# Single-bank score tiles, halved squares and a new instruction order in an attention and MLP kernel

## The chip, the cores and the metric

The kernel runs on one core of one Trainium2 chip. Its time is the device time of one launch in microseconds (us), the median of several executions. Five engines work side by side, each through its own list of instructions in order: TensorE for matmuls (PE; its weight loads are PEld), VectorE (DVE), ScalarE (ACT), GpSimd (POOL) and SyncE (SP, which here only issues DMAs). An instruction that needs another engine's result waits for a semaphore, and what stands behind it on its engine waits too. [...]

## The reference

Attention with RMS-normalized q and k, for 8 batches of 12 heads, 448 tokens and head size 64; then an MLP on the 3584 tokens of width 768, with inner width 2048:

```python
q_n, k_n = rmsnorm(q, g_q), rmsnorm(k, g_k)        # x / sqrt(mean(x*x) + 1e-6) * g
attn = softmax(scale * q_n @ k_n.T)
x = (attn @ v).transpose(0, 2, 1, 3).reshape(3584, 768)
h = x @ w_in                                       # 768 x 2048
g = h * (1 / (1 + exp(-1.702 * h)))
out = g @ w_out                                    # 2048 x 768
```

Inputs and output are float32; the kernel multiplies in bfloat16.

## The kernel before, in words

**The pieces of work.** Heads are taken in pairs, six pairs per batch, numbered i = 0 to 47. For a pair, `load` fetches q, k and v rows by DMA (112 partitions; 224 KB each). `square` (L1044) squares the rows, on ACT or on GpSimd, `reduce` (L1051) sums the squares on DVE, `seed` and `rsqrt` (L1073, L1084) make the inverse root on DVE and GpSimd, and `norm` (L1097) scales the rows, on GpSimd or DVE. `vcast` (L1104) makes v in bfloat16. The rows are transposed, on PE (`turn_pe`, with `take_q` and `take_k` behind it) or by a DMA (`turn_dma`, with `scale_q` behind it: the KQ scalings). Then `score` (L1157) multiplies q by k into a score tile, `expo` (L1173) takes exponentials on ACT, `values` (L1183) multiplies them by v into the one `o` bank, with a column of ones that gives the sum, and `divide` (L1196) divides on DVE, which frees the `o` bank. The quotient is transposed into `xt`, on PE (`back_pe`, `take_x`) or by DMA.

For a batch, `first` (L1398) multiplies `xt` by w_in in 16 blocks of 128 columns, `tanh` (L1411, ACT) and `gate` (L1415, DVE) form g, and the second product, by w_out, is done per pair of batches and 128 tokens. Most of it is done as a Strassen-like scheme of seven products (P1 to P7) of operands that `add_up` (L1485, DVE) has summed; `product` (L1492) is one of them, 8 matmuls 384 wide. `copy_out` (ACT) and `copy_out_v` (DVE) scale a sum into SBUF, `add_out` (L1513, DVE) adds a further product, and `store` (L1445) writes it out, on SP's queue or, for the very last tokens, partly on ACT's. The last two batches' first products are done jointly in the same manner, after attention has ended: `joint_product` (L1738), `part_copy`, `part_add`, `gelu` (L1750 to L1764).

**PSUM.** Two score tiles `sc0`, `sc1` of two banks each, one `o` bank and three `w` banks. Before attention ends, the products share `w` banks only. Once it has ended (task `late`, L1842), the four halves of the two score tiles are put to use as four more banks for the products: `banks` is a list of seven from which `bank()` takes what the planner chose.

**The order.** It isn't written out by hand. Each piece of work is a task in `_Order` (from L27), with an engine, an assumed duration, what it depends on, the slots that it takes ("w", "sc", "o", "osb", "sums"), and a key. `run` plays the tasks through on the assumed durations; whenever an engine is free, it emits the ready task of the lowest key. The emission order on each engine is the program; the chip then runs it with semaphores, whatever the real durations. Keys are in a table `KEYS`, the earliest times of loads in `AT`, and `ON` names the tasks that use their second engine (GpSimd for a square, DVE for a norm, ACT for a KQ scaling). `FINAL` (L1537) is the list of the last products, ending with E8 and E4.

**Zero matmuls.** `fill` (L1018) is called ahead of each PE task with the idle time that the plan sees, and puts in matmuls of zeros, 256 columns wide, into the `w` bank not yet in use; it is switched off when the number of `w` banks grows (`widen`), which is when the first projection begins. There are 92 of them.

Of the kernel before, what the change touches and what calls it, by code (L numbers as in the profile page):

```python
# [26 lines left out]
class _Order:  # L27
# [36 lines left out]
    def run(self):  # L64
# [60 lines left out]
        while emitted < len(self.tasks):  # L125
            for eng, q in ready.items():
                while q and free[eng] <= now:
# [24 lines left out]
                    for name, n in best.widen or ():  # L152
                        self.slots[name][0] = n
                        self.fill = None
# [71 lines left out]
    'Lg': 0.22, 'g': 55.26, 'gT': 30.23, 'gG': 70, ('L', 0, 0): 0.37, ('L', 0, 1): 0.13, ('L',  # L226
    0, 2): 17.62, ('S', 0, 0): -40, ('R', 0, 0): 17.66, ('S', 0, 1): -37.12, ('R', 0, 1): 56.72,
    ('Q', 0): -38.13, ('N', 0, 0): -12.18, ('N', 0, 1): 14.86, ('V', 0): 56.98, ('T', 0, 0):
    12.94, ('T', 0, 1): -21.61, ('KQ', 0): 70, ('K', 0): 65.88, ('L', 1, 0): 7.61, ('L', 1, 1):
    7.62, ('L', 1, 2): 1.46, ('S', 1, 0): -39.85, ('R', 1, 0): 30.33, ('S', 1, 1): 0.22, ('R',  # L230
    1, 1): 30.34, ('Q', 1): -39.63, ('N', 1, 0): -13.05, ('N', 1, 1): -14.01, ('V', 1): 70,
    ('T', 1, 0): 6.24, ('T', 1, 1): 13.57, ('KQ', 1): 69.99, ('K', 1): 18.15, ('L', 2, 0): 17.9,
    ('L', 2, 1): 38.14, ('L', 2, 2): -5.44, ('S', 2, 0): -33.18, ('R', 2, 0): 13.95, ('Q', 2):
    -38.13, ('N', 2, 0): -29.82, ('N', 2, 1): -13.56, ('V', 2): -13.57, ('T', 2, 0): -21.6,
    ('T', 2, 1): 16.29, ('KQ', 2): 70, ('K', 2): 62.97, ('L', 3, 0): 41.06, ('L', 3, 1): 9.24,
    ('L', 3, 2): 43.15, ('S', 3, 0): -38.12, ('R', 3, 0): 65.09, ('Q', 3): -34.18, ('N', 3, 0):
    -12.87, ('N', 3, 1): -26.87, ('V', 3): 69.95, ('T', 3, 0): 11.11, ('T', 3, 1): 11.69, ('KQ',
    3): 56.73, ('K', 3): 20.74, ('L', 4, 0): 18.91, ('L', 4, 1): -19.56, ('L', 4, 2): 15.83,
    ('S', 4, 0): 0.95, ('R', 4, 0): 67.9, ('Q', 4): -34.27, ('N', 4, 0): 20.82, ('N', 4, 1):
    -17.57, ('V', 4): -11.3, ('T', 4, 0): -3.0, ('T', 4, 1): -2.97, ('KQ', 4): -11.72, ('K', 4):  # L240
    69.48, ('L', 5, 0): 22.36, ('L', 5, 1): -18.14, ('L', 5, 2): 17.7, ('S', 5, 0): -10.17,
    ('R', 5, 0): 70, ('Q', 5): -37.13, ('N', 5, 0): 24.39, ('N', 5, 1): -26.27, ('V', 5): 15.01,
    ('T', 5, 0): -12.89, ('T', 5, 1): -11.92, ('KQ', 5): 60.78, ('K', 5): 59.31, ('L', 6, 0):
    15.46, ('L', 6, 1): -18.15, ('L', 6, 2): -3.94, ('S', 6, 0): -16.71, ('R', 6, 0): -7.33,
    ('N', 6, 0): -16.52, ('N', 6, 1): -10.48, ('V', 6): 6.19, ('T', 6, 0): 10.28, ('T', 6, 1):
    23.05, ('KQ', 6): 0.72, ('K', 6): 3.84, ('L', 7, 0): 38.54, ('L', 7, 1): 15.83, ('L', 7, 2):
    -4.28, ('S', 7, 0): -24.47, ('R', 7, 0): 3.83, ('N', 7, 0): 6.2, ('N', 7, 1): 6.21, ('V',
    7): -9.14, ('T', 7, 0): -39.98, ('T', 7, 1): -38.38, ('KQ', 7): -6.41, ('K', 7): 0.85, ('L',
    8, 0): -1.72, ('L', 8, 1): 11.56, ('L', 8, 2): 10.08, ('S', 8, 0): -24.91, ('R', 8, 0):
    -6.41, ('Q0', 8): 32.07, ('Q', 8): 28.01, ('N', 8, 0): 5.71, ('N', 8, 1): -8.0, ('V', 8):  # L250
    -12.74, ('T', 8, 0): 13.67, ('T', 8, 1): 47.73, ('KQ', 8): 0.59, ('K', 8): -0.49, ('L', 9,
    0): -10.64, ('L', 9, 1): 10.1, ('L', 9, 2): 45.1, ('S', 9, 0): 26.07, ('R', 9, 0): 6.92,
    ('N', 9, 0): -6.74, ('N', 9, 1): -10.36, ('V', 9): 13.05, ('T', 9, 0): 44.4, ('T', 9, 1):
    5.86, ('KQ', 9): 18.33, ('K', 9): -6.72, ('L', 10, 0): -12.09, ('L', 10, 1): 38.53, ('L',
    10, 2): 9.25, ('S', 10, 0): -24.13, ('R', 10, 0): 4.83, ('N', 10, 0): -4.44, ('N', 10, 1):
    -6.78, ('V', 10): -10.35, ('T', 10, 0): 26.56, ('T', 10, 1): 9.68, ('KQ', 10): 37.6, ('K',
    10): 0.88, ('L', 11, 0): -9.36, ('L', 11, 1): -16.64, ('L', 11, 2): -26.52, ('S', 11, 0):
    -10.35, ('R', 11, 0): -6.55, ('Q0', 11): -11.27, ('Q', 11): -18.03, ('N', 11, 0): 0.65,
    ('N', 11, 1): 1.38, ('V', 11): -4.19, ('T', 11, 0): 7.07, ('T', 11, 1): -11.77, ('KQ', 11):
    -12.98, ('K', 11): 30.09, ('L', 12, 0): -5.03, ('L', 12, 1): -35.43, ('L', 12, 2): -20.7,  # L260
    ('S', 12, 0): 46.96, ('R', 12, 0): -6.72, ('N', 12, 0): 36.31, ('N', 12, 1): 26.26, ('V',
    12): 24.25, ('T', 12, 1): 68.34, ('KQ', 12): 9.67, ('L', 13, 0): -35.76, ('L', 13, 1):
    -13.65, ('L', 13, 2): -12.08, ('S', 13, 0): 19.67, ('R', 13, 0): -11.91, ('N', 13, 0):
    -5.48, ('N', 13, 1): 10.21, ('V', 13): 35.01, ('T', 13, 1): 50.14, ('KQ', 13): 29.64, ('L',
    14, 0): -28.77, ('L', 14, 1): -33.63, ('L', 14, 2): -23.28, ('S', 14, 0): -32.54, ('R', 14,
    0): -6.68, ('Q0', 14): 14.59, ('Q', 14): 42.35, ('N', 14, 0): 42.36, ('N', 14, 1): 17.66,
    ('V', 14): 52.1, ('T', 14, 1): 68.52, ('KQ', 14): 30.13, ('L', 15, 0): -10.21, ('L', 15, 1):
    -21.03, ('L', 15, 2): -10.86, ('S', 15, 0): 21.43, ('R', 15, 0): 0.71, ('N', 15, 0): 17.26,
    ('N', 15, 1): -14.78, ('V', 15): 17.91, ('T', 15, 1): 69.44, ('KQ', 15): -3.57, ('L', 16,
    0): -10.28, ('L', 16, 1): -2.32, ('L', 16, 2): -23.28, ('S', 16, 0): 27.33, ('R', 16, 0):  # L270
    31.04, ('N', 16, 0): 15.29, ('N', 16, 1): -10.33, ('V', 16): 21.01, ('T', 16, 1): 64.02,
    ('KQ', 16): 17.87, ('L', 17, 0): -11.13, ('L', 17, 1): 4.77, ('L', 17, 2): -26.53, ('S', 17,
    0): 55.55, ('R', 17, 0): 34.56, ('Q0', 17): 38.18, ('Q', 17): -14.77, ('N', 17, 0): 17.28,
    ('N', 17, 1): -14.76, ('V', 17): 21.85, ('T', 17, 1): 54.96, ('KQ', 17): 18.94, ('L', 18,
    0): -10.24, ('L', 18, 1): -18.65, ('L', 18, 2): 60.64, ('S', 18, 0): 8.24, ('R', 18, 0):
    -0.11, ('N', 18, 0): 18.68, ('N', 18, 1): 18.68, ('V', 18): 22.61, ('T', 18, 1): 19.87,
    ('KQ', 18): 13.42, ('L', 19, 0): 65.93, ('L', 19, 1): 68.74, ('L', 19, 2): 57.38, ('S', 19,
    0): 68.06, ('R', 19, 0): 19.11, ('N', 19, 0): 13.7, ('N', 19, 1): 18.69, ('V', 19): 24.79,
    ('T', 19, 1): 27.31, ('KQ', 19): 20.75, ('L', 20, 0): 49.44, ('L', 20, 1): 49.43, ('L', 20,
    2): 18.36, ('S', 20, 0): 47.45, ('R', 20, 0): -7.1, ('Q0', 20): 17.6, ('Q', 20): 17.74,  # L280
    ('N', 20, 0): 18.63, ('N', 20, 1): 19.13, ('V', 20): 10.89, ('T', 20, 1): 23.29, ('KQ', 20):
    19.79, ('L', 21, 0): 49.88, ('L', 21, 1): 54.32, ('L', 21, 2): 21.44, ('S', 21, 0): 32.39,
    ('R', 21, 0): 24.48, ('N', 21, 0): 40.58, ('N', 21, 1): 20.67, ('V', 21): 9.73, ('T', 21,
    1): 20.87, ('KQ', 21): 24.17, ('L', 22, 0): 54.3, ('L', 22, 1): 45.12, ('L', 22, 2): 23.02,
    ('S', 22, 0): 9.37, ('R', 22, 0): 18.5, ('N', 22, 0): 40.59, ('N', 22, 1): 22.19, ('V', 22):
    19.73, ('T', 22, 1): 21.96, ('KQ', 22): 25.44, ('L', 23, 0): 20.78, ('L', 23, 1): 17.14,
    ('L', 23, 2): 21.94, ('S', 23, 0): 19.12, ('R', 23, 0): 19.39, ('Q0', 23): 37.96, ('Q', 23):
    58.13, ('N', 23, 0): 42.56, ('N', 23, 1): 21.37, ('V', 23): 12.12, ('T', 23, 1): 19.53,
    ('KQ', 23): 27.37, ('L', 24, 0): 27.32, ('L', 24, 1): 23.46, ('L', 24, 2): 19.89, ('S', 24,
    0): 15.36, ('R', 24, 0): 20.63, ('N', 24, 0): 24.12, ('N', 24, 1): 26.27, ('V', 24): 9.99,  # L290
    ('T', 24, 1): 14.3, ('KQ', 24): 34.67, ('L', 25, 0): 21.43, ('L', 25, 1): 21.42, ('L', 25,
    2): 19.52, ('S', 25, 0): 22.92, ('R', 25, 0): 29.14, ('N', 25, 0): 20.8, ('N', 25, 1):
    30.38, ('V', 25): 13.2, ('T', 25, 1): 24.46, ('KQ', 25): 27.87, ('L', 26, 0): 21.46, ('L',
    26, 1): 21.76, ('L', 26, 2): 19.55, ('S', 26, 0): 11.3, ('R', 26, 0): 3.81, ('Q0', 26):
    10.43, ('Q', 26): 11.29, ('N', 26, 0): 33.52, ('N', 26, 1): 32.94, ('V', 26): 36.87, ('T',
# [562 lines left out]
def kernel(  # L858
# [138 lines left out]
    ps_sc = pool("ps_sc", 1, space=PSUM)  # L997
    ps_o = pool("ps_o", 1, space=PSUM)
    ps_w = pool("ps_w", 1, space=PSUM)

    od = _Order()
    for name, n in (("sc", 2), ("o", 1), ("w", 2), ("th", 3), ("osb", 5)):
        od.slot(name, n)
# [931 lines left out]
```

## Time and the profile before

| | |
|---|---|
| median of 3 executions | 423.13 us (422.65 to 424.16) |
| profiled execution | 425.17 us |
| its span, first to last instruction | 423.4 us |
| PE's idle share | 4% |
| mean granted clock of PE | 0.996 |
| traffic with HBM | 45.61 MB read, 11.01 MB written |

The span is what the trace covers; the execution's own time is 1.8 us more. In the trace, a line of the timeline gives the start and length in us, the engine, the source line (L1403 is line 1403 of the kernel), the operation, what it writes and reads, and in brackets how long the engine stood idle ahead of it and what ended that. A group of equal instructions in a row is one line with xcount. The groups of the page give the busy time, the mean in ns and the idle time before them. The costliest on PE are the first product (L1403, 121.2 us in 672 matmuls), the second (L1497) and the attention products (L1170, L1191: 1280 matmuls of 65 columns in 58.7 us); on ACT the exponentials (L1178, 168 of 915 ns); on DVE the reductions (L1058, 50 of 1171 ns), the gates (L1425, 96 of 615 ns) and the divisions (L1202, 96 of 425 ns); on GpSimd the norms (L1100, 61 of 1115 ns) and squares (L1046, 27.1 us in 14).

### The profile page before, as it was taken

The page shows a single profiled execution, that of the slowest core. Times are in us where ns is not written, and L with a number is a line of the kernel's source. Part 1 is how long each engine was busy: PE and PEld are TensorE (multiplying, and loading weights), DVE is VectorE, ACT ScalarE, POOL GpSimd, SP SyncE. Part 2 cuts the span into 40 slices and gives each one's busy share as a digit, 9 for nine tenths or more (in the row PEclk, how much of TensorE's full clock was granted, in tenths as well). Part 3 has the DMA queues.
Part 4 walks back from the last instruction along what each step waited for, and adds up shares of the span by engine and source line. Part 5 has one row for each costly group of instructions (what it writes and reads, how often), then busy time and mean ns, then how long its engine had stood idle before and what let it go on. Part 6 is the DMA issues. An engine that isn't in the chain of part 4 may idle for free.

```text
span 423.4 us, 10002 instructions
## 1 busy us (share of the span) xinstructions
PE 406.6 (96%) x3845; PEld 238.7 (56%) x3845; DVE 324.7 (77%) x647; ACT 295.4 (70%) x435; POOL 173.4 (41%) x252
## 2 busy tenths in 40 slices
PE   7899989998999999999999999999999999999995
PEld 5658866554555555554555554555555654545663
DVE  4877878879999888888788869998666897557432
ACT  3898585889878578867897768858887625763221
POOL 4965986581545175807537364662300000000000
PEclk9999998999999999999999999999999999999999
DMA  9999999966385899695974878546441231001323
GB/s 207 245 245 245 256 238 249 239 165 132 88 185 128 161 227 212 119 240 148 212 171 119 179 198 223 130 111 161 112 110 33 70 77 49 3 0 24 89 76 112
DMA packets 101556, 63.38 MB, mean 150 GB/s; under 512 B 54916, under 2 KB 101508, under 8 KB 101508
## 3 DMA queue, kind: packets, MB, share of 16 engines
q1 hardware_dynamic: 93712, 55.88, 56.0%
q0 software_dynamic: 7296, 6.29, 9.1%
q8 instruction: 30, 0.49, 0.5%
q10 hardware_dynamic: 500, 0.57, 0.4%
q14 instruction: 18, 0.15, 0.1%
HBM read 45.61 MB, written 11.01 MB: 134 GB/s over the span
## 4 chain that ended last, share of the span: by engine, by line
PE 69%; DMA 13%; DVE 11%; ACT 3%; issue 2%; SPq 0%; DVEq 0%; ACTq 0%
PE w L1403 21%; PE w L1497 18%; PE o L1191 10%; PE sc L1170 8%; DMA rows<-in_q_dram 6%; DMA rows<-in_k_dram 5%; PE sc L1497 5%; PE w L1433 4%; PE sc L1744 2%; DMA late<-in_k_dram 2%; PE w L1744 2%; DVE late L1488 1%; DVE obs L1202 1%; DVE ssq L1058 1%; DVE att L1758 1%
## 5 line engine op out<-in xcount | busy, mean ns | idle before, releaser
L1178 ACT ACTIVATE att<-sc 112x896 bf16<-112x896 f32 x168 | 145.8, 915 | 37.2 <-PE sc L1170 36.5
L1403 PE MATMUL w<-xt,w_in_s 128*128 128x448 bf16 (+1 forms) x672 | 121.2, 327 | 0.7 <-DVE g L1425 0.4
L1403 PEld LDWEIGHTS <-w_in_s 128*128 128x128 bf16 x672 | 61.2, 98 | 44.8 <-issue 9.9
L1191 PEld LDWEIGHTS <-att 112*128 112x128 bf16 x1536 | 62.7, 98 | 30.0 <-issue 8.2
L1100 POOL TENSOR_TENSOR row<-rows,rs 112x512 bf16<-112x512 f32 x61 | 66.7, 1115 | 11.1 <-DMA qk<-row 9.2
L1413 ACT ACTIVATE th<-w 128x448 f32<-128x448 f32 x96 | 51.8, 546 | 24.3 <-PE w L1403 23.4
L1425 DVE SCALAR_TENSOR_TENSOR g<-th,w 128x448 bf16<-128x448 f32 x96 | 57.9, 615 | 12.2 <-ACT th L1413 11.8
L1058 DVE TENSOR_REDUCE ssq<-sq 112x16 f32<-112x1024 f32 (+1 forms) x50 | 58.4, 1171 | 10.9 <-ACT sq L1049 7.8
L1191 PE MATMUL o<-vx,att 112*128 112x65 bf16 x1280 | 58.7, 194 | 4.2 <-DVE obs L1202 3.8
L1113 POOL TENSOR_TENSOR vx<-rows,ones 112x512 bf16<-112x512 f32 x20 | 21.9, 1095 | 66.9 <-PE o L1191 59.2
L1170 PE MATMUL sc<-qk 64*128 64x448 bf16 (+1 forms) x360 | 47.3, 342 | 0.4 <-DVE qk L1130 0.2
L1046 POOL TENSOR_TENSOR sq<-rows 112x1024 f32<-112x1024 f32 (+1 forms) x14 | 27.1, 1934 | 43.2 <-DMA rows<-in_k_dram 17.3
L1202 DVE TENSOR_TENSOR obs<-o,rcp 112x256 bf16<-112x256 f32 x96 | 40.8, 425 | 3.3
L1497 PEld LDWEIGHTS <-g 128*128 128x128 bf16 x296 | 27.2, 98 | 21.1 <-issue 4.7
L1497 PEld LDWEIGHTS <-late 128*128 128x128 bf16 x304 | 27.5, 97 | 19.2 <-issue 2.9
L1049 ACT ACTIVATE sq<-rows 112x1024 f32<-112x1024 f32 (+1 forms) x32 | 32.3, 1016 | 5.5 <-DMA rows<-in_q_dram 2.8
L1497 PE MATMUL w<-w_out_s,g 128*128 128x384 bf16 x152 | 28.7, 326 | 0.0
L1497 PE MATMUL w<-w_out_s,late 128*128 128x384 bf16 x152 | 28.6, 326 | 0.0
L1201 DVE RECIPROCAL rcp<-o 112x4 f32<-112x4 f32 x96 | 17.0, 177 | 14.8 <-PE o L1191 14.5
L1100 DVE TENSOR_TENSOR row<-rows,rs 112x512 bf16<-112x512 f32 x27 | 22.7, 841 | 2.2 <-POOL rs L1093 2.0
L1497 PE MATMUL w<-late 128*128 128x384 bf16 x128 | 24.3, 326 | 0.1
L1180 ACT ACTIVATE att<-sc 112x896 bf16<-112x896 f32 x24 | 20.5, 916 | 1.2 <-PE sc L1170 1.1
(130 smaller groups left out, 505.5 us busy)
## 6 DMA issues: line engine op xcount, KB each, us to landing
rows<-in_q_dram SPq DMA_DIRECT2D x44, 224.0 KB, 3.8
rows<-in_k_dram SPq DMA_DIRECT2D x43, 224.0 KB, 4.3
rows<-in_v_dram SPq DMA_DIRECT2D x42, 224.0 KB, 3.4
w_in_s<-in_moe_w_in_dram POOLq DMA_DIRECT2D x4, 768.0 KB, 17.0
w_out_s<-in_moe_w_out_dram POOLq DMA_DIRECT2D x4, 768.0 KB, 21.2
out_dram<-osb SPq DMA_DIRECT2D x10, 168.0 KB, 2.9
out_dram<-osb SPq DMA_DIRECT2D x14, 120.0 KB, 2.1
out_dram<-osb SPq DMA_DIRECT2D x11, 144.0 KB, 2.6
```

Source lines behind the costliest of these rows:

```text
L1046: nc.gpsimd.tensor_tensor(out=sq[i % N_SQ][:SS, part], in0=raw[turn(i, N_RAW, K_RAW)][:SS, part], in1=raw[turn(i, N_RAW, K_RAW)][:SS, part ...
L1049: nc.scalar.activation(out=sq[i % N_SQ][:SS, part], in_=raw[turn(i, N_RAW, K_RAW)][:SS, part], func=ACT.Square)
L1058: nc.vector.reduce_sum(out=ssq_of[g0][:SS, i - g0, part], in_=sq[i % N_SQ][:SS, part], axis=AX.X)
L1100: eng.tensor_tensor(out=row_ring[i % N_QKN][:SS, gi].rearrange("p n (h d) -> p h n d", h=2), in0=raw[turn(i, N_RAW, K_RAW)][:SS, gi], in1= ...
L1170: nc.tensor.matmul(sc[:, hp, j * SH:j * SH + n], lhsT=qkw[r, k0:k0 + WIN], rhs=qk[r, 0, qs], start=True, stop=True)
L1178: nc.scalar.activation(out=att[:SS, t, :, :S], in_=sc, func=ACT.Exp)
L1191: nc.tensor.matmul(os_[u, w][:, x, :], lhsT=att_of(u)[:SS, kc, hp, qs * SS:qs * SS + WIN], rhs=vx_ring[turn(i, N_V, K_V)][:SS, hp, kc, :], ...
L1202: nc.vector.tensor_tensor(out=to[:SS, :, w, :] if h is None else to[:SS, :2].rearrange("p n h d -> p (n h) d"), in0=o[:SS, :, :D], in1=rcp ...
L1403: nc.tensor.matmul(gps[b, m][:, j * SH:j * SH + n], lhsT=w_in_s[:, ki, f * 128:(f + 1) * 128], rhs=xT[b][:, ki, lo:lo + n], start=(ki == 0 ...
L1413: nc.scalar.activation(out=th[:, :], in_=gps[b, m][:, :S], func=ACT.Tanh, scale=0.851)
L1425: nc.vector.scalar_tensor_tensor(out=g_of[b // 2][:, f:f + len(g), lo:lo + n], in0=view(ths.pop((b, m))[:, :]), scalar=1.0, in1=view(gps.p ...
L1497: nc.tensor.matmul(held[to], lhsT=lhs[:, ko, :], rhs=y[:, ko, :], start=first and ko == 0, stop=ko == NK - 1, skip_group_check=not first)
```

## The change

1. **Banks.** The score tiles' pool is closed when attention ends, and four tiles of one bank each, `b0` to `b3`, take the place of the four halves (`part_banks`). The pool of the score tiles is made last, so that it can be closed first.
2. **Zero matmuls.** `fill` is no longer switched off. The matmuls are 240 wide; until 14 us of planned time and until 45 us the number follows the idle time, with other divisors; later it puts some in only where the plan sees more than 0.9 us of idle time, and into an open bank. The built program has 103.
3. **Squares.** A square on GpSimd is two instructions of 112x512 (q and k apart) in place of one of 112x1024. The pairs whose square is on GpSimd are 15 and a half of one before, 16 after.
4. **Last product.** E4 becomes E9: the last product is done in two column halves of 192, 8 matmuls each; the first half is copied out by ACT and the second by DVE, and each is stored by itself.
5. **A new order.** All of `KEYS`, `AT` and `ON` have other values. Counted in the built programs: norms on DVE 27 before and 23 after, on GpSimd 61 and 65; V conversions on DVE 17 and 19, on GpSimd 20 and 18 (of the main buffers); KQ scalings on DVE 22 and 24, on ACT 14 and 12; copies of products on DVE 20 and 16 (osb), and eight more on ACT.
6. `joint_product` looks up its operand only for the product that it issues; the work is the same.

The diff without the tables:

```diff
@@ -151,7 +151,6 @@
                     for name, n in best.widen or ():
                         self.slots[name][0] = n
-                        self.fill = None
                     if eng == "PE" and self.fill:
                         self.fill(now - free[eng], now)
...
-    ps_sc = pool("ps_sc", 1, space=PSUM)
     ps_o = pool("ps_o", 1, space=PSUM)
     ps_w = pool("ps_w", 1, space=PSUM)
+    scores = ctx.enter_context(ExitStack())
+    ps_sc = scores.enter_context(tc.tile_pool(name="ps_sc", bufs=1, space=PSUM))
...
+    def part_banks():
+        scores.close()
+        ps_b = pool("ps_b", 1, space=PSUM)
+        banks[3:] = [ps_b.tile([128, 512], FP32, tag=f"b{j}", name=f"b{j}") for j in range(4)]
+
...
-        n = idle * FILL / 213 if now < 14000.0 else idle * FILL_GAPS / 110
-        for _ in range(int(n)):
-            nc.tensor.matmul(banks[2][:, :256], lhsT=ident[:, :], rhs=zeros[:, :],
+        if now < 14000.0:
+            n = idle * FILL / 200
+        elif now < 45000.0:
+            n = idle * FILL_GAPS / 103
+        else:
+            n = (idle - 400.0) * FILL_GAPS / 103 if idle > 900.0 else 0.0
...
+        for _ in range(n):
+            nc.tensor.matmul(banks[j][:, :240], lhsT=ident[:, :], rhs=zeros[:, :240],
                              start=True, stop=True)
...
         if ("S", i, part.start) in ON:
-            nc.gpsimd.tensor_tensor(out=sq[i % N_SQ][:SS, part], in0=raw[turn(i, N_RAW, K_RAW)][:SS, part],
-                                    in1=raw[turn(i, N_RAW, K_RAW)][:SS, part], op=ALU.mult)
+            for g in range(part.start, part.stop):
+                nc.gpsimd.tensor_tensor(out=sq[i % N_SQ][:SS, g], in0=raw[turn(i, N_RAW, K_RAW)][:SS, g],
+                                        in1=raw[turn(i, N_RAW, K_RAW)][:SS, g], op=ALU.mult)
             return
...
-                   alt=("POOL", 1700 / len(parts) + 200, False),
+                   alt=("POOL", 1050 * (part.stop - part.start), False),
...
-    def store(bp, tm, hf):
+    def store(bp, tm, hf, part=None):
...
-                in_=osb[r:r + n, :HALF])
+                in_=osb[r:r + n, part])
...
+    def product_part(to, x, y, cols):
+        lhs = sum_of[x] if x in sum_of else tokens(*x)
+        for ko in range(NK):
+            nc.tensor.matmul(held[to][:, cols], lhsT=lhs[:, ko, :], rhs=y[:, ko, cols],
+                             start=False, stop=ko == NK - 1, skip_group_check=True)
+
+    def copy_part(frm, bp, tm, hf, cols, by_v):
+        to, x = half_of(bp, tm, hf)[:, cols], held[frm][:, cols]
+        if by_v:
+            nc.vector.tensor_scalar(out=to, in0=x, scalar1=SCALE[bp], scalar2=None, op0=ALU.mult)
+        else:
+            nc.scalar.mul(to, x, SCALE[bp])
...
-                   "E5 C7 E6 C4 C3 E7 E8 E4")
+                   "E5 C7 E6 C4 C3 E7 E8 E9")
...
+        def p4_last():
+            nonlocal done, last
+            hf = HALF // 2
+            for j in range(2):
+                cols = slice(j * hf, (j + 1) * hf)
+                od.add((*P(4), j), "PE", 8 * 82,
+                       lambda cols=cols: product_part(a, A(3), T4, cols), now_key(),
+                       deps=[last, X(3)] + term(3), lat=250)
+                last = (*P(4), j)
+                done += 8 * 82
+                name = ("U", *at[1], 0, 0)[:5 - j]
+                od.add(name, "ACT" if j == 0 else "DVE", 310 if j == 0 else 320,
+                       lambda j=j, cols=cols: copy_part(a, *at[1], 0, cols, j), now_key() - 3,
+                       deps=[last], takes=("osb", [("D", *at[1], 0)]) if j == 0 else None)
+                od.add(("D", *at[1], 0, j) if j == 0 else ("D", *at[1], 0), "SP", 900,
+                       lambda cols=cols: store(*at[1], 0, cols), now_key() + 1,
+                       deps=[name], moves=300.0)
...
-            od.add("late", "none", 0, lambda: None, 0, widen=[("w", len(banks))],
+            od.add("late", "none", 0, part_banks, 0, widen=[("w", len(banks))],
```

## The prediction

> **What bounds the kernel now.** I read the page first, then busy time by stage, then the timeline where a stage loses time. The page's first part:
>
> ```profile
> PE 406.6 (96%) x3845; PEld 238.7 (56%) x3845; DVE 324.7 (77%) x647; ACT 295.4 (70%) x435; POOL 173.4 (41%) x252
> ```
>
> PE is the bound, and the change keeps its work (3753 matmuls in both built programs, fillers apart), so only PE's idle and slow time can be won. The stages (start:end, length, then PE, PEld, DVE, ACT, POOL busy, granted clock, DMA share, GB/s):
>
> ```profile
> 0.00:60.00 60.00, 54.41 (x678) 41.83 (x679) 44.05 (x99) 44.35 (x66) 43.14 (x67) 1.00 1.12 239
> 60.00:70.00 10.00, 7.89 (x74) 5.48 (x72) 7.71 (x14) 7.76 (x12) 9.23 (x15) 0.83 1.22 247
> 70.00:335.00 265.00, 261.74 (x2582) 145.28 (x2581) 220.47 (x448) 206.82 (x289) 120.89 (x171) 1.00 0.69 157
> 335.00:418.80 83.80, 82.52 (x518) 46.11 (x516) 52.45 (x89) 36.03 (x70) 0.18 (x1) 1.00 0.20 54
> 418.80:423.40 4.60, 0.02 (x1) 0.00 (x0) 0.00 (x0) 0.49 (x1) 0.00 (x0) 0.98 0.33 99
> ```
>
> At a saturated 239 to 247 GB/s, loads set the pace to about 60 us (fillers hide idle PE time). From 70 us PE is 98.6% busy; the tail is 4.6 us. 60 to 70 us is the worst:
>
> ```profile
> 58.49 1.06 ACT L1049 ACTIVATE sq<-late 112x1024 f32<-112x1024 f32 x1 [1.06 <-DMA late<-in_k_dram]
> 61.33 1.22 DVE L1058 TENSOR_REDUCE ssq<-sq 112x16 f32<-112x1024 f32 x1 [0.46 <-ACT sq L1049]
> 62.47 0.17 DVE L1201 RECIPROCAL rcp<-o 112x4 f32<-112x4 f32 x1
> 63.16 0.56 PE L1191 MATMUL o<-vx,att 112*128 112x65 bf16 x12 [2.11 <-DVE obs L1202]
> 64.13 1.81 PE L1403 MATMUL w<-xt,w_in_s 128*128 128x224 bf16 x12
> ```
>
> A k load lands late; the squares wait, the reduce waits for them, and the divide that frees the one `o` bank is queued behind the reduce on DVE. PE stands 2.11 us: in PE's order nothing lies between two `o` blocks here. Then the clock is halved for 3.4 us (granted 0.60 over 64 to 68 us; twelve L1403 matmuls take 1.81 us, 1.31 elsewhere): about 1.7 us lost.
>
> In two later holes a GpSimd square holds up a DVE instruction:
>
> ```profile
> 191.90 1.89 POOL L1046 TENSOR_TENSOR sq<-rows 112x1024 f32<-112x1024 f32 x1 [10.18 <-DVE ssq L1058]
> 192.08 1.76 DVE L1079 TENSOR_SCALAR rs<-ssq 112x48 int32<-112x48 int32 x1
> 194.91 0.68 PE L1191 MATMUL o<-vx,att 112*128 112x65 bf16 x16 [0.88 <-DVE obs L1202]
> ...
> 280.35 2.51 POOL L1046 TENSOR_TENSOR sq<-rows 112x1024 f32<-112x1024 f32 x1 [2.99 <-DMA rows<-in_k_dram]
> 281.02 2.38 DVE L1488 TENSOR_TENSOR late<-g,late 128x1024 bf16<-128x1024 bf16 x1
> 284.01 0.68 PE L1191 MATMUL o<-vx,att 112*128 112x65 bf16 x16 [0.63 <-DVE obs L1202]
> ```
>
> Undisturbed, L1079 takes 0.19 us and L1488 0.69; here each ends with the square, and the next divide and PE are late.
>
> In the joint stage (from 335 us) PE loses 3.3 us in twelve pieces of 0.2 to 0.6:
>
> ```profile
> 359.15 0.52 ACT L1755 COPY osb<-sc 128x448 f32<-128x448 f32 x1
> 359.73 0.73 PE L1744 MATMUL sc<-xt,rows 128*128 128x448 bf16 x3
> 359.73 0.85 PEld L1744 LDWEIGHTS <-rows 128*128 128x128 bf16 x5 [0.35 <-issue]
> ```
>
> These matmuls begin as the copy ends (359.15+0.52 = 359.67); in the built program they write one half of the two-bank score tile, and the copy reads the other.
>
> [...]
>
> **Single banks after attention.** The built program of before has 16 waits in the joint and final stages whose named reader is in the other half of the tile; after has none, and PE's waits in that region fall from 70 to 63. Between the last write of a tile and its next one, PE has 0 to 0.65 us of other work eleven times; after, 0.65 at the least and mostly 2.27. A reader needs about 0.6 us (copy 0.52 and its signal), so about eight of the twelve holes, at 0.25 each, go: **−2.0**. Both ends: 0, if the next wait (part_add at L1758, which waits for the ACT copy) takes their place, and −3.3, all of it. The other edit in that function, a product operand chosen when emitted, moves no work: 0.
>
> **Squares in two.** 15 squares of 112x1024 (2003 ns mean) and one half become 32 halves; the one half in the trace took 1.04 us. GpSimd: 16×2.08 against 15×2.00+1.04, +2 us, and +4×1.1 for norms moved to it, at 41% busy: hidden by its idle time of 250 us. A blocked DVE instruction waits at most 1.04 us instead of 2.0: the holes of 0.88+0.16 and 0.63+0.18 us shrink by about 0.6 each: **−1.2**, bounds −1.9 (both gone) and +0.5 (the other places[...]).
>
> **New order.** DVE gives up four norms (0.84 each) and four copies (0.56) and takes two V reductions (0.68) and two KQ scalings (0.44 at most): 3 to 4 us less, at 77% busy; ACT takes eight copies (0.49) and gives up two of 14 KQ scalings (0.68). Neither bounds. PE work between consecutive `o` blocks falls below 0.5 us at four places before (0 at the stall; 0.38 at 95 and at 229 us), at one after, early: **−0.4** (0.2 to 0.4 us at each of two, part of it taken by waits elsewhere). At 60 us 1.55 us of other PE work now lies between, but it waits for exps and tanhs that ACT runs behind the same two squares, and the last k load of the pair is SP load 41, not 40: 224 KB at 245 GB/s, 0.9 us later. Of 1.55 minus 0.9 I take **−0.4**. The half-clock window follows or not by chance: half of 1.7, **−0.9** (0 to −1.7). The first score comes about 1 us earlier (two first norms on DVE at 0.84 instead of GpSimd at 1.1), but the loads set the pace to 58 us: 0. A searched order has holes of its own that order lists do not show; between 70 and 335 us before loses 3.3 us, and I allow half of that again: **+1.5** (0 to +4).
>
> **Zero matmuls.** 92×256 columns become 103×240, 100 of them before about 45 us, where PE waits anyway (0.1 us each hidden by load waits; if a load came sooner, up to 0.3 us late). Three are at about 96 us, where PE stands 0.74 us for transposes: **0**. The first waits on ACT, so a late ACT there would pass through: +0.3 at worst.
>
> **Last product in halves.** Eight matmuls of 384 (1.30 us) become sixteen of 192 (1.32). In the built program the ACT copy of half one waits for all sixteen, and the DVE copy of half two for the ACT copy: same bank. From 0.49 us (384 wide) and 0.53 (448) I estimate 0.33 for ACT; from 0.555, 0.36 for DVE. The second large store is issued about 0.3 us later (two issues of 0.38 on ACT's queue), with half the bytes (168 KB land in 2.3 us, 72 in 1.9): −0.2. **+0.1**, bounds −0.5 and +0.5.
>
> **Sum.** −2.0−1.2−0.4−0.4−0.9+1.5+0.1 = −3.3 us in the span. The profiled execution took 425.17 us around a span of 423.4; the runs' median, 423.13, is lower than either sum suggests, so I take the difference from the median: **419.8 us**.
>
> **The rivals.**
> A, the forecast: 419.8; own range 417.5 to 421.5; chance 0.46.
> C, the block at 60 us dissolves: the 2.11 us wait and the half-clock window both go, −3.8 in place of −1.3: 417.3, and 416.5 with fewer new holes. For it: the 1.55 us between the `o` blocks. Against: the later k load. 0.13.
> B, holes move: the joint stage's waits pass to the DVE adds (half of −2.0 lost), and the new order's holes are +3 instead of +1.5: 419.8+1.0+1.5 = 422.3. For it: PE at 98.6% leaves little to win. 0.20, of which 0.07 is faster by over 0.3%.
> D, slower: at about 60 us the late k load (0.9) holds ACT's squares, the exps and tanhs behind them (two of 0.92) come late, PE has only their products left, and a second half-clock window (1.7) follows. That is 4.4 us against −2.0 from the sum without its 60 us terms: 425.5. It decides from 3.3 us of added stall there (2.0 won elsewhere plus 1.27). For it: ACT is in order and both squares stand together; DMA is saturated until 70 us. Against: PE has more work queued, DVE some 3 us less. 0.21.
> That the edits don't do what they say holds for the tail alone (halves without overlap), and is priced.
>
> **How the numbers follow.** 0.3%, 1.27 us, is about what a measurement of this kernel can tell from no change; same is 421.9 to 424.4. Faster: 0.46+0.13+0.07 = 0.66; same 0.13; slower 0.21. The range goes from 416.0, just below C, to 425.0, within D; about 0.05 lies below and 0.11 above.
>
> **What would show it.** Joint stage: no matmul that writes a score bank waits for a copy of another, and PE loses about 1.3 us from 335 us on instead of 3.3. Squares of 1.04 us, and no DVE instruction over about 1.1 us longer than usual behind one. Around 60 us: a PE wait of about 1.5 us, and the granted clock shows whether the half-clock window came. At the end: about 4.7 us from the last matmul. The prediction is wrong if loads end later than 60 us by several load times, if the middle stage loses over 5 us, or if the joint stage's waits come back on DVE.

## The result

The kernel after takes 417.88 us (median of 4, 417.36 to 418.74), the kernel before beside it 423.64: a ratio of 0.986, interval 0.9818 to 0.9902. Measured once more, in the study below, it took 420.20 (median of 6) against 424.01, a ratio of 0.9909 (0.9890 to 0.9928). The two intervals share 0.989 to 0.990; 0.9 to 1.4% faster, 4 to 6 us, is what the two together support.

The profiled execution took 417.67 us, its span is 415.9. PE is busy for 404.9 us of it (97%). Its worst stretch before, from 60 to 70 us (start:end, length; PE, PEld, DVE, ACT and POOL busy, granted clock, DMA share, GB/s):

```profile
60.00:70.00 10.00, 9.68 (x120) 6.88 (x117) 8.99 (x19) 8.66 (x14) 8.46 (x12) 1.00 1.22 249
```

PE is busy 9.68 us there instead of 7.89, at full clock instead of 0.83. The timeline there (here and below, lines between the ones shown are left out):

```profile
57.59 2.00 ACT L1068 ACTIVATE sq<-late 112x1024 f32<-112x1024 f32 x2
58.68 2.35 DVE L1077 TENSOR_REDUCE ssq<-sq 112x16 f32<-112x1024 f32 x2
59.28 0.68 PE L1210 MATMUL o<-vx,att 112*128 112x65 bf16 x16
59.80 1.31 PE L1422 MATMUL w<-xt,w_in_s 128*128 128x224 bf16 x12
61.15 0.42 DVE L1221 TENSOR_TENSOR obs<-o,rcp 112x256 bf16<-112x256 f32 x1
61.25 0.56 PE L1189 MATMUL sc<-qk 64*128 64x448 bf16 x4
61.74 0.56 PEld L1210 LDWEIGHTS <-att 112*128 112x128 bf16 x16 [0.37 <-DVE obs L1221]
```

Neither these reduces nor ACT's squares show a wait. Twelve first-product matmuls (1.31 us, where twelve took 1.81 at 64 us in before) and four score matmuls (0.56) now lie between two `o` blocks, and the second block waits 0.37 us instead of 2.11.

The same DVE instruction as at 192 us before, behind a square in two halves of 1.02 us each (187.95 to 189.99), and the `o` block after it:

```profile
188.13 0.91 DVE L1098 TENSOR_SCALAR rs<-ssq 112x48 int32<-112x48 int32 x1
189.76 0.68 PE L1210 MATMUL o<-vx,att 112*128 112x65 bf16 x16
```

It takes 0.91 us instead of 1.76 (0.19 undisturbed), and PE doesn't wait. The place in the joint stage that was at 359 us:

```profile
353.61 0.53 ACT L1808 COPY osb<-b 128x448 f32<-128x448 f32 x1
353.98 0.73 PE L1797 MATMUL b<-xt,rows 128*128 128x448 bf16 x3
```

The matmuls into one bank begin 0.16 us before the copy of another ends (353.61+0.53). And the tail:

```profile
412.02 0.33 ACT L1532 ACTIVATE att<-b 128x192 f32<-128x192 f32 x1 [2.13 <-PE b L1524]
412.38 0.87 ACTq L1475 DMA_DIRECT2D out_dram<-att  x2
412.39 0.36 DVE L1530 TENSOR_SCALAR att<-b 128x192 f32<-128x192 f32 x1 [1.12 <-ACT att L1532]
```

The halves follow one another, as the built program said: all matmuls, ACT's copy, DVE's copy. Still the span ends 2.65 us after the last issue (413.25 to 415.9), where it ended 3.64 after it before (419.76 to 423.4).

**Lost time by stage.** For comparing fourteen traces I use one number: the length of a stage less what its real matmuls take when they follow each other without a gap (0.19 us for 448 columns and 0.1625 for 384, as far as their starts lie apart in the trace of the kernel after; 0.039 for 65, the mean of fifteen steps of 0.033 within an `o` block and one of 0.127 to the scores behind it; a wide score matmul, which has only 64 rows and starts within some 4 ns of a second one in the trace, counts half; about 379 us in all). Stages are cut at equal amounts of that work: 34, 46 and 300 us, which is about 55, 70 and 335 us of time. Other weights move a whole column of the table; the differences between its rows hardly change. In us, one profiled execution each:

| kernel | loads (to 34) | block (34 to 46) | middle (to 300) | joint, final | tail | span |
|---|---|---|---|---|---|---|
| before | 21.5 | 3.7 | 11.3 | 3.4 | 4.6 | 423.4 |
| after | 21.6 | 0.4 | 10.0 | 1.1 | 3.9 | 415.9 |
| after_again | 23.3 | 0.6 | 10.5 | 1.0 | 3.9 | 418.3 |
| a_two_bank | 23.0 | 0.7 | 10.9 | 3.5 | 3.9 | 420.9 |
| a_whole_sq | 22.2 | 0.7 | 11.3 | 1.1 | 4.4 | 418.5 |
| a_quarter_sq | 21.1 | 0.6 | 10.0 | 1.0 | 3.9 | 415.7 |
| a_e4 | 23.9 | 0.4 | 10.4 | 1.1 | 4.2 | 418.9 |
| a_no_late_zero | 20.7 | 0.5 | 11.1 | 1.0 | 3.9 | 416.2 |
| a_order_alone | 21.6 | 1.0 | 10.6 | 3.5 | 4.7 | 420.3 |
| b_one_bank | 21.3 | 3.5 | 12.3 | 1.7 | 4.5 | 422.2 |
| b_half_sq | 20.5 | 1.1 | 10.2 | 3.4 | 4.2 | 418.3 |
| b_work_before_o | 21.3 | 2.6 | 12.0 | 3.4 | 4.6 | 422.9 |
| b_zeros_in_stall | 22.2 | 5.8 | 11.5 | 3.4 | 4.6 | 426.4 |
| b_square_first | 21.7 | 12.3 | 13.1 | 3.4 | 4.6 | 434.0 |

From before to after: block −3.3, middle −1.3, joint and final −2.3, tail −0.7, loads +0.1. But these are single executions. The same program in `after` and `after_again` differs by 2.4 us, 1.7 of it in the load stage; the eight traces with the new order lost 20.7 to 23.9 us there. The block of before has a half-clock stretch (granted 0.50 from 64.81 to 68.23 us) worth about 1.7 us; only 37 of before's 102 runs have a mean granted clock under 0.998. The profiled execution of before was 0.9 to 1.5 us above four of the kernel's medians (2.0 above that of its first three runs), that of after near the low end of its ten runs. Of the 7.5 us between the two spans, then, 1.5 to 3.5 are the executions.

### The profile page after: what moved, and what is told of

It reads as the page before. It is cut to its first block, busy times and chain, and to the rows that moved or that the text cites. A ratio compares the mean times of both kernels' runs of the same rounds, so it can differ in the third digit from the quotient of the medians.

```text
span 415.9 us, 10074 instructions
## 1 busy us (share of the span) xinstructions
PE 404.9 (97%) x3864; PEld 240.0 (58%) x3864; DVE 319.8 (77%) x644; ACT 297.0 (71%) x437; POOL 175.5 (42%) x270
## 4 chain that ended last, share of the span: by engine, by line
PE 80%; DMA 7%; DVE 4%; ACT 3%; issue 2%; POOL 2%; SPq 0%; DVEq 0%; POOLq 0%; ACTq 0%
PE w L1422 22%; PE w L1517 21%; PE o L1210 11%; PE sc L1189 9%; PE b L1517 4%; PE b L1797 4%; DMA rows<-in_q_dram 4%; PE w L1797 4%; PE w L1452 3%; DMA late<-in_v_dram 3%; ACT att L1199 2%; POOL row L1119 1%; DMA rows<-in_k_dram 1%; DVE late L1508 1%; ACT L902 1%
## 5 line engine op out<-in xcount | busy, mean ns | idle before, releaser
L1119 POOL TENSOR_TENSOR row<-rows,rs 112x512 bf16<-112x512 f32 x65 | 69.0, 1083 | 31.8 <-DMA qk<-row 14.7
L1132 POOL TENSOR_TENSOR vx<-rows,ones 112x512 bf16<-112x512 f32 x18 | 19.0, 1057 | 54.5 <-PE o L1210 41.8
L1517 PEld LDWEIGHTS <-late 128*128 128x128 bf16 x304 | 28.0, 98 | 21.4 <-issue 4.4
L1065 POOL TENSOR_TENSOR sq<-rows 112x512 f32<-112x512 f32 x28 | 28.6, 1039 | 24.5 <-DMA rows<-in_q_dram 10.5
L1517 PEld LDWEIGHTS <-g 128*128 128x128 bf16 x288 | 26.3, 98 | 19.3 <-issue 3.6
L1517 PE MATMUL w<-w_out_s,late 128*128 128x384 bf16 x144 | 27.0, 326 | 0.1
L1517 PE MATMUL w<-late 128*128 128x384 bf16 x136 | 25.6, 326 | 0.1
L1109 POOL TENSOR_TENSOR t<-rs 112x48 f32<-112x48 f32 x28 | 9.5, 339 | 29.4 <-DVE rs L1098 28.3
## 6 DMA issues: line engine op xcount, KB each, us to landing
w_out_s<-in_moe_w_out_dram POOLq DMA_DIRECT2D x4, 768.0 KB, 20.5
```

Source lines behind the costliest of these rows:

```text
L1119: eng.tensor_tensor(out=row_ring[i % N_QKN][:SS, gi].rearrange("p n (h d) -> p h n d", h=2), in0=raw[turn(i, N_RAW, K_RAW)][:SS, gi], in1= ...
L1517: nc.tensor.matmul(held[to], lhsT=lhs[:, ko, :], rhs=y[:, ko, :], start=first and ko == 0, stop=ko == NK - 1, skip_group_check=not first)
```

## The experiments

Names in a_ are the kernel after with something undone, names in b_ the kernel before with something done. All ratios are to the kernel before on the same chip; its median was 424.04, 424.31 and 424.01 us in the three groups (40, 51 and 11 runs), so 0.1% is 0.42 us. The third group (a_quarter_sq, a_no_late_zero, b_square_first and the kernel after again) ran on another chip than the first two, so kernels of different groups are compared by their ratios.

**Banks, undone and done alone.** (A bank is here a tile of 128x512 float32 in PSUM, where matmuls leave their sums.)

```diff
-            od.add("late", "none", 0, part_banks, 0, widen=[("w", len(banks))],
+            od.add("late", "none", 0, lambda: None, 0, widen=[("w", len(banks))],
```

a_two_bank:

> The kernel after, with the four halves of the two-bank score tiles in place of the four single-bank tiles; nothing else changes, and the order of every engine stays. Built, it has 19 waits of product matmuls on a reader of the other half (the kernel after: 0, before: 21). Theory of the banks: the holes of 0.2 to 0.3 us come back in the joint and final stages, PE loses about 3.0 us there instead of 1.3, time +1.5 to +2.0 us against the kernel after. Rival (the new order alone keeps readers ahead of writers): PE has other work between the two writes, and the time moves by less than 0.5 us.

b_one_bank has the opposite edit, with the score pool made last:

> The kernel before with single-bank tiles once attention has ended, and nothing else. Theory of the banks: PE's loss from 335 us to its last matmul falls from 3.3 to about 1.5 us, time -1.8 against the kernel before, all of it after 343 us. Rival (the new order is needed for it): under -0.5. The stall at 60 us is untouched: about 2.1 us of waiting for the divided o block, and the half clock after it when it comes.

a_two_bank took 422.18 us, ratio 0.9946 (0.9926 to 0.9967). By the ratios that is 1.6 us over the second measurement of the kernel after (0.9909) and 3.6 over the first (0.986); joint and final stages lost 3.5 us instead of 1.0. Its timeline where the kernel after has no wait:

```profile
357.00 0.53 ACT L1808 COPY osb<-sc 128x448 f32<-128x448 f32 x1
357.59 0.73 PE L1797 MATMUL sc<-xt,rows 128*128 128x448 bf16 x3
```

b_one_bank took 421.87 us, 0.9938 (0.9918 to 0.9958), 2.2 us under before by the medians and 2.6 by the ratio; joint and final stages 1.7 instead of 3.4. At the same point of the program:

```profile
359.36 0.53 ACT L1761 COPY osb<-b 128x448 f32<-128x448 f32 x1
359.73 0.73 PE L1750 MATMUL b<-xt,rows 128*128 128x448 bf16 x3
```

With the halves, the matmuls begin 0.06 us after the copy ended (357.53); with banks of their own, 0.16 before it ends (359.89). So what the theory of the banks expects shows in both orders, at about the forecast size. The new order isn't needed for it.

**Squares.** a_whole_sq puts the single instruction of 112x1024 back, b_half_sq splits it in the kernel before:

```diff
-            for g in range(part.start, part.stop):
-                nc.gpsimd.tensor_tensor(out=sq[i % N_SQ][:SS, g], in0=raw[...][:SS, g], in1=raw[...][:SS, g], op=ALU.mult)
+            nc.gpsimd.tensor_tensor(out=sq[i % N_SQ][:SS, part], in0=raw[...][:SS, part], in1=raw[...][:SS, part], op=ALU.mult)
```

> The kernel after with each square on GpSimd as one instruction of 112x1024 (about 1.95 us) instead of two of 112x512; order as in the kernel after. [...] DVE instructions that start inside a square wait up to 1.9 us instead of 0.85; summed excess of DVE instructions over their usual length rises from 8.1 to 10 us or more, two or three of them delay a divide, +0.5 to +1.2 us. Rival (the order moved the squares away from what DVE is late with): the excess rises, the time does not (within 0.5 us).

> The kernel before with its squares on GpSimd as two instructions of 112x512; order as before. [...] the holes of PE at 194.9 us (0.88 us) and 284.0 us (0.63 us) shrink to 0.3 us or less, -1.2 us in all. Rival: [...] the time moves by less than 0.5 us.

In the old order the halves win: b_half_sq took 422.12 us, 0.9953 (0.9929 to 0.9977), 1.9 under before. The middle stage falls from 11.3 to 10.2 (three other traces with whole squares in this order have 11.5 to 12.3). PE's waits of over 0.1 us between 70 and 335 us add up to 3.2 to 3.7 us in those four traces and to 1.7 here: the holes at 194.9 and 284.0 us are gone. The DVE instruction that took 1.76 us behind the square at 192 us takes 0.91 here, as in the kernel after. By the lines of before it ended 0.05 us after that square (193.84 against 193.79), and the one at 281 us 0.54 after its own (283.40 against 282.86).

In the new order the wait comes back with whole squares, and one `o` block with it:

```profile
189.32 1.76 DVE L1097 TENSOR_SCALAR rs<-ssq 112x48 int32<-112x48 int32 x1
191.69 0.68 PE L1209 MATMUL o<-vx,att 112*128 112x65 bf16 x16 [0.57 <-DVE obs L1220]
```

That hole is 0.6 us. PE's waits in the middle stage add up to 2.5 us with whole squares (a_whole_sq, and a_order_alone below) and to 1.5 to 2.8, mean 1.9, in six traces with halves. In time nothing shows: a_whole_sq took 420.18, ratio 0.9906 (0.9877 to 0.9934), beside 0.9909 for the kernel after; the intervals are too wide to exclude a microsecond. What DVE loses behind a whole square is as expected (1.76 us against 0.91); how much of it reaches PE depends on the order (0.88 us in before, 0.57 here), and here the rival (the order keeps the squares off what is urgent) is nearer.

Quarters, the same cut once more (a loop over the two heads inside, four instructions of 112x256):

> The kernel after with each square on GpSimd as four instructions of 112x256 instead of two of 112x512; order as in the kernel after. [...] a DVE instruction waits at most about 0.5 us behind a square instead of 0.85, but what is left of the waits in the kernel after is mostly behind norms (1.04 us), and GpSimd takes some 16 x 0.1 us longer in squares: -0.4 to 0 us. Rival (every halving wins as much as the first, 1.3 us): -1 us or more, which would beat the kernel after. Rival (one instruction's fixed cost is large, and squares become late): slower by 0.5 us or more.

419.00 us, 0.9888 (0.9857 to 0.9918), which overlaps the kernel after widely; the middle stage lost 10.0 us, as in the kernel after. Nothing speaks for a further gain of 1 us in that stage, and nothing for a loss; a few tenths can't be told.

**The last product whole.**

```diff
-                   "E5 C7 E6 C4 C3 E7 E8 E9")
+                   "E5 C7 E6 C4 C3 E7 E8 E4")
```

> The kernel after with its last product whole (8 matmuls of 384, one ACT copy, one store) instead of in two column halves. My forecast for the halves was +0.1 us; the two traces show the time from PE's last matmul to the end of the span at 4.58 us before and 3.91 after. Theory (the last transfer, half as long, lands sooner): that time is 4.4 to 4.6 us here, +0.5 to +0.7 against the kernel after. Rival (the tail differs for another reason, such as what else is on the DMA queues): 3.9 us here too.

419.66 us, 0.9883 (0.9851 to 0.9916): no slower in the time, against the expectation. The tail of its trace is 4.2 us, between the expectation (4.4 to 4.6) and its rival (3.9), and the span ends 3.3 us after the last issue (415.58 to 418.9). Over all fourteen traces the tail is 4.2 to 4.7 us, 4.5 in the mean, in the eight with one last store, and 3.9 to 4.4, mean 4.0, in the six with two. So the halves are worth about 0.5 us, by the traces; six runs are too few to see it in the time.

**Zero matmuls off again** once the banks grow:

```diff
                         self.slots[name][0] = n
+                        self.fill = None
```

> The kernel after with the zero matmuls switched off once the number of banks for products grows, as in the kernel before: the three at about 92 us go, the early ones stay. Theory: they stand inside a wait for transposes (0.9 us without work) and cost nothing: 0, within 0.3 us. Rival (they keep the clock from being halved after that wait): half-clock runs as in the kernel before, +0.5 us or more at the median.

419.22 us, 0.9883 (0.9857 to 0.9910), no run with a clock under 0.999. From the start of the `o` block to the transposes behind it, it is 1.42 us in the kernel after (91.69 to 93.11), with three zero matmuls between, and 1.42 us here (91.54 to 92.96), with none. The three zero matmuls do nothing for the time.

**The order alone**: two-bank halves, whole squares, E4 and no late zero matmuls, in the order of the kernel after.

> The new order without the other edits: the kernel after with two-bank halves, whole squares, the last product whole, and no zero matmuls after the first projection has begun (the early ones as in the kernel after). If the edits' gains are those of the traces (banks 2.0, squares up to 1.2, tail 0.7), it runs 3 to 4 us slower than the kernel after, about 421 us, still some 3 us under the kernel before, by the block at 60 us. Rival (the order carries nearly all): under 2 us slower than the kernel after. Rival (the order by itself is worth nothing): 423 us or more.

422.55 us, 0.9956 (0.9935 to 0.9976): by the ratios 1.9 us under the kernel before and 2.0 (second measurement) to 4.1 us (first) over the kernel after. It lies between the first two expectations. So the order, with its early zero matmuls, which were not tried apart, carries a third to a half of the gain. Between its trace and that of before the middle stage falls by 0.7 us and the block from 3.7 to 1.0; but 1.7 of the 3.7 is the half-clock stretch, and b_half_sq, in the old order and without it, lost 1.1 there. How much of the order's 1.9 us is made in the block is not settled by single traces. The load stage lost 22.2 us in the mean of eight traces of the new order and 21.4 in that of six of the old, while single traces of either spread by 1.7 to 3.2 us.

**What the block at 60 us is.** The prediction had said: a late k load holds ACT's squares, and with them DVE's reduce and the divide; PE has nothing between two `o` blocks; and the half clock comes after that wait. Two experiments on PE's part of that. The first put zero matmuls into PE's wait, the second moved real work there:

```diff
     def values(u, w, x):
+        if calls[0] == 52:
+            for _ in range(18):
+                nc.tensor.matmul(banks[0][:, :256], lhsT=ident[:, :], rhs=zeros[:, :], start=True, stop=True)
+        calls[0] += 1
```

> The kernel before with 18 zero matmuls, 256 wide (about 1.95 us), put into PE's order just ahead of the o block that waits 2.11 us at 61 us; they write a bank that is free there. The wait for the divide stays, so PE's real work is as late as before, but PE is not idle. Theory of the clock: the granted clock stays at 1.0 over 62 to 70 us, and the real matmuls from 63 to 70 us run at full speed, -1.5 to -1.7 us where the half clock would have come. Rival (the half clock does not come from this idle time): granted 0.6 to 0.7 somewhere in 62 to 70 us all the same, time unchanged or up to +0.2.

```diff
     def values(u, w, x, again=False):
+        if not again:
+            calls[0] += 1
+            if 53 <= calls[0] <= 55:
+                later.append(lambda: values(u, w, x, True))
+                return
...
     def first(b, m, kis):
...
+        todo = later[:]
+        later.clear()
+        for k in todo:
+            k()
```

(The scores between are put off in the same way.)

> The kernel before with three tasks exchanged in PE's order at 61 us: the next 12 first-product matmuls (1.3 us) and 4 score matmuls (0.55 us) go ahead of the o block that waits for the divide. Nothing else changes. Theory (the block at 60 us is PE having nothing between two o blocks): the wait of 2.11 us falls to 0.5 us or less and no half clock follows, -1.6 us from the wait and up to -1.7 from the clock. Rival (the late loads set the pace of the stage): the lost time shows up at the next scores or o block, under -0.7 us.

b_zeros_in_stall took 425.65 us, 1.0033 (1.0014 to 1.0052), slower; b_work_before_o 424.58, 1.0015 (0.9991 to 1.0039), no gain. Neither could show what it was made for, for the same reason. In the first the zero matmuls, in the second the twelve moved matmuls wait as long as the `o` block did:

```profile
63.92 3.79 PE L1189 MATMUL w<-zeros,ident 128*128 128x256 bf16 x18 [2.23 <-DVE g L1432]
```

```profile
63.25 1.31 PE L1417 MATMUL w<-xt,w_in_s 128*128 128x224 bf16 x12 [2.42 <-DVE g L1443]
```

Their bank is freed by a gate on DVE, and the gate is queued behind the same reduces as the divide (the expectation took the bank of the zero matmuls to be free). So this work could not help PE there. Other work was not tried. The zero matmuls then ran after the wait, 3.79 us at the halved clock (granted 0.83 in the mean of 60 to 70 us), so this kernel says nothing on what the clock would do if PE were kept busy; that stays untested.

Why is DVE late? In before two chains lead to the divide, and the prediction shows the lines of one. The other:

```profile
55.73 1.91 POOL L1046 TENSOR_TENSOR sq<-rows 112x1024 f32<-112x1024 f32 x1
57.67 1.22 DVE L1058 TENSOR_REDUCE ssq<-sq 112x16 f32<-112x1024 f32 x1 [1.64 <-POOL sq L1046]
60.25 1.05 ACT L1049 ACTIVATE sq<-late 112x1024 f32<-112x1024 f32 x1
```

DVE's reduce at 57.67 us had waited 1.64 us for a square on GpSimd, which stood behind a V conversion and the issue of a w_out load. ACT's two squares began with the late k load, the second ended at 61.30 us, and the last reduce ahead of the divide waited 0.46 us for it. The last experiment puts that square ahead of both:

```diff
     def square(i, part):
         if ("S", i, part.start) in ON:
+            n_sq[0] += 1
             nc.gpsimd.tensor_tensor(...)
+            if n_sq[0] == 6:
+                for k in held_back:
+                    k()
...
     def vcast(i):
...
+        n_v[0] += 1
+        if n_v[0] == 6:
+            held_back.append(cast)
+        else:
+            cast()
...
     def load_out(c):
+        if c == 1:
+            held_back.append(lambda: load_now(c))
+            return
+        load_now(c)
```

> The kernel before with one change in GpSimd's order at 54 us: the square that DVE waits 1.64 us for at 57.7 us goes ahead of a V conversion (1.04 us) and the issue of a w_out load (0.96 us). It can start when its buffer comes free, at about 54.5 instead of 55.7 us. Theory (the stall at 61 us is DVE's, which is behind since that wait, and with it the divides and gates): DVE's reduce starts at about 56.5 instead of 57.7 us, PE's wait of 2.11 us falls to about 1, no half clock, -1 to -2 us. Rival (the late k load and the two squares on ACT set the time of the divide): the wait stays at 1.8 us or more, under -0.4 us.

434.69 us, 1.0238 (1.0205 to 1.0272), much slower, by a side effect of the edit. Up to 64 us the trace shows what was asked, and one thing more:

```profile
56.92 1.22 DVE L1065 TENSOR_REDUCE ssq<-sq 112x16 f32<-112x1024 f32 x1 [0.69 <-POOL sq L1049]
57.56 1.06 ACT L1056 ACTIVATE sq<-late 112x1024 f32<-112x1024 f32 x1
60.41 1.22 DVE L1065 TENSOR_REDUCE ssq<-sq 112x16 f32<-112x1024 f32 x1 [0.29 <-ACT sq L1056]
62.23 0.56 PE L1205 MATMUL o<-vx,att 112*128 112x65 bf16 x12 [0.99 <-DVE obs L1216]
```

The first reduce waits 0.69 us instead of 1.64, and PE 0.99 instead of 2.11. Then the moved V conversion, now emitted behind a later load into its buffer, waits 8.05 us for that load, until 64.94 (so this pair's product uses other v rows, and the output is not the reference's), the norms behind it on GpSimd come late, and PE stands 8.44 us until 73.75. The total is void; the first lines are not.

But they don't single out the square. ACT's first square no longer waits for the k load, either (1.06 us in before): the edit also put off all three w_out loads, which before issues from 54.7 to 59.4 us, to 65.9 us, so other traffic ran beside that load. In b_half_sq, where the loads came sooner, both waits shrink together, too:

```profile
55.62 1.22 DVE L1059 TENSOR_REDUCE ssq<-sq 112x16 f32<-112x1024 f32 x1 [0.58 <-POOL sq L1047]
60.99 0.56 PE L1192 MATMUL o<-vx,att 112*128 112x65 bf16 x12 [0.94 <-DVE obs L1203]
```

In four of the six traces of the old order DVE waits 1.38 to 1.64 us for GpSimd's square, ACT 0.65 to 1.06 us for the k load, and PE 1.83 to 2.42 us. In the other two it is 0.58 and 0.69 us, nothing, and 0.94 and 0.99 us. In all six, DVE's last wait ahead of the divide is for ACT's second square (0.21 to 0.46 us). An estimate from the lines of before: with GpSimd's square alone a microsecond earlier, the reduce at 61.33 us would still wait for ACT; with the k load alone earlier, DVE would be busy until 60.86, and gain about half a microsecond. So the late k load, which the prediction named, was the last link in before, and DVE's delay from GpSimd stood close behind it. No run has one without the other.

The new order does something else. a_order_alone, between two `o` blocks:

```profile
59.38 0.68 PE L1210 MATMUL o<-vx,att 112*128 112x65 bf16 x16
61.70 0.42 DVE L1221 TENSOR_TENSOR obs<-o,rcp 112x256 bf16<-112x256 f32 x1
61.81 0.56 PE L1189 MATMUL sc<-qk 64*128 64x448 bf16 x4 [0.60 <-ACT att L1197]
62.30 0.56 PEld L1210 LDWEIGHTS <-att 112*128 112x128 bf16 x16 [0.37 <-DVE obs L1221]
```

From the end of the first block to the end of the division it is 2.06 us (60.06 to 62.12), no less than in before (61.05 to 63.09, 2.04 us). But the twelve first-product matmuls and the four score matmuls, 1.9 us, lie between, their banks come free in time or nearly so, and PE waits 0.60 and 0.37 us. Over the eight traces of the new order this release takes 1.58 to 2.06 us and PE waits 0.37 to 0.97. So here PE work is the cure, and the division is little sooner; in b_work_before_o work of the same kind hung on DVE itself.

**The kernel after again**, beside the rest:

> The kernel after itself, as the base for the kernels made from it, with many runs beside the kernel before. Expected as in its first four runs, 417.9 us, 1.4% under before; granted clock at 0.998 or more in nearly all runs, where the kernel before has 0.993 to 0.997 in 35 of 91.

420.20 us, 0.9909 (0.9890 to 0.9928): less than the first four runs showed, with a granted clock of 0.998 or more in every run. a_quarter_sq, a_no_late_zero and a_e4 have lower medians, but none is told apart from it.

## Why the prediction held, and where it didn't

The time forecast, 419.8 us, is 1.9 over the first median and 0.4 under the second; the own range of case A holds both. As a difference it was −3.3 us; by the ratios the two measurements are −5.9 and −3.9. Step by step, against the table:

- **Single banks, −2.0:** measured −2.3 in the traces (3.4 to 1.1), −2.2 to −2.6 us as b_one_bank alone, −1.6 (against the second measurement) as a_two_bank undone. The size was right, and matmuls into one single bank do begin before the copy of another ends (0.16 us in both traces shown); the waits did not pass to the DVE adds (case B).
- **Squares in two, −1.2:** the wait behind the square at 192 us shrank as said (1.76 to 0.91 us); that it lasts at most as long as the square was my estimate from two pairs of lines. In the old order that was worth 1.9 us of time, 1.7 of it in PE's waits in the middle stage; in the new one 0.5 us in PE's waits and nothing that the times show. The step took the holes of the old order as they stood; in the new order with whole squares, no wait is left near the hole at 284 us, and the other costs PE 0.57 us instead of 0.88.
- **The block at 60 us, −0.4 and −0.9:** measured −3.3 between the traces, −2.7 for the order alone, 1.7 of either the half clock of that one execution of before. The mechanism of the wait was right: PE work between the `o` blocks covers a division that comes hardly sooner. The term that was mis-sized is the 0.9 us taken off that work for the late k load: in none of the eight traces of the new order do ACT's two squares wait for a load, and PE's wait fell from 2.11 to between 0.37 and 0.97 us. Case C was nearer for this block; rival D, which rested on the same load, did not come.
- **The half clock, half of 1.7:** right that not every run has it. In before, 37 of 102 runs have a mean granted clock under 0.998; in the kernel after and the five variants of it that keep any of its edits, none of 53; in a_order_alone 4 of 22. Its price is less certain: such runs are slower by 2.2 us at the median in b_half_sq (7 of 15), 2.3 in a_order_alone and 2.5 in b_zeros_in_stall (13 of 22), by 0.1 in b_work_before_o (9 of 14) and by 0.7, 0.0 and 1.1 in the three groups of before. A run's mean doesn't say where the stretch lay: in the trace of b_work_before_o it lay at 11 to 14.5 us (granted 0.51), in the load stage, and the block ran at full clock. Whether that explains the prices is open.
- **Holes of the new order, +1.5, and `o` blocks, −0.4:** wrong sign in the middle stage, which lost 11.8 us in the mean of four traces of the old order with whole squares and 11.0 in the two of the new. A hole of its own the new order does have, 1.02 to 1.04 us in all eight of its traces; in the kernel after:

```profile
223.17 1.53 DVE L1508 TENSOR_TENSOR late<-g 128x1024 bf16<-128x1024 bf16 x1
225.91 0.68 PE L1210 MATMUL o<-vx,att 112*128 112x65 bf16 x16 [1.03 <-DVE obs L1221]
```

  The addition at 223.17 takes 1.53 us instead of 0.68, and a scaling before it 1.11 instead of 0.33, while GpSimd works on three norms (220.62 to 224.14 us); the divide is queued behind them. Against it stand holes of before at 104.5 and 229 us that are gone. Norms in halves were not tried.
- **Tail, +0.1:** −0.5 by the means. The order of copies was right; the term that was mis-sized is the last transfer: I took 0.2 us for half the bytes; the span ends 0.7 (against a_e4) to 1.0 us (against before) sooner after the last issue.
- **Zero matmuls, 0:** measured 0.00 us between the two marks.

The sum came out as near as it did partly by luck: a gain too small (block) and a loss that did not come (holes) stood against a gain that was mostly gone in the new order (squares). Two small slips changed nothing: the matmuls apart from the zeros are 3753 before but 3761 after, the eight more being those of the halved last product, and PE's 98.6% from 70 us to its last matmul is 98.7% by the lines shown. Of the base, the prediction said that the profiled execution lay above the median and took differences from the median; the two spans alone would have said 7.5 us.

## What to carry to other kernels

When PE waits for a release by another engine, there are two ways out: let the release come sooner, or give PE work meanwhile. For the second, look first at who frees the bank that the work writes: in the old order the moved matmuls hung on the same late DVE as the `o` block, in the new order the same kind of work covers a release that takes as long (2.06 us in a_order_alone, 2.04 in before). For the first, follow every chain that leads to the release, not only the longest wait: here one ran over GpSimd and one over a load and ACT, and by the lines of before they ended within half a microsecond of each other. In a_two_bank, matmuls into one half of a two-bank tile began 0.06 us after the copy of the other had ended, and in b_one_bank, with single banks, 0.16 us before the copy ended: cut such tiles to single banks when the use changes. Two edits that aim at the same waits need not add up: measure each alone and each undone.

## What the runs showed of the hardware

Half-clock stretches of PE (granted 0.50 over 3.4 us) followed waits of 2.11, 1.83 and 2.23 us in the traces of before, b_one_bank and b_zeros_in_stall; after 2.42 us in b_work_before_o PE stayed at full clock from 60 to 70 us. The length of the wait alone doesn't tell these four traces apart. Two executions of the kernel after differ by 1.7 us in the load stage, at 240 and 247 GB/s over the first 60 us, and the eight kernels with its order by 3.2, which makes single spans poor evidence for changes of 1 us. Splitting the last store in two ended the program 2.65 us after its last issue instead of 3.3 (a_e4) to 3.6 (before), though the second half was issued 0.5 us later than the first.
